# Joining the bf16 products of neighbouring tile pairs in a Strassen-form GEGLU kernel

## Chip, cores, metric

One core of one Trainium2 chip. The metric is the device time of one execution in microseconds (us). Every run quoted here is in the fast state or a single look (state unknown), at a granted clock of 0.999 or 1.0. The **span** of a trace, from its first to its last instruction, is 1.7 to 2.1 us shorter than the time of the same execution in nearly every run.

## The reference, cut

```python
# x 1 x 2048 x 1024, w_gate and w_up 1024 x 3584, w_down 3584 x 1024, all bf16
def reference(x, w_gate, w_up, w_down):
    return (_gelu(x @ w_gate) * (x @ w_up)) @ w_down
```

## The kernel before

The tokens are done in two halves of 1024. A half has a *pair stage* (gate and up products, gelu, multiply) and a *down stage* (times `w_down`). Both replace eight block products by seven, M1 to M7, in the manner of Strassen (Winograd's form). In the pair stage M1 and M2 take bf16 operands as they are; the other five take sums of blocks, kept as 32-bit floats (float32r, printed as f32). Each product is done twice, j = 0 for gate and j = 1 for up, with 4 matmuls of 128x512 each time. One pass handles a *pair* of tiles of the inner dimension; the first half has 12 pairs (numbers 2 to 13), the second 14 (0 to 13).

The kernel uses eight banks of PSUM, the memory that PE writes its products to, in pairs:

```python
PB, VB, QB, RB = (0, 1), (2, 3), (4, 5), (6, 7)

# pair_quads, the seven products; cut: the definitions of mm, prep, add_m5
for j in range(2):                                             # M1, bf16
    mm(PB[j], j, block(key, j, 0, 0), b11, True)
    act(nc.scalar.copy(out=banks[QB[j]][:], in_=banks[PB[j]][:]))
for j in range(2):                                             # M5, f32
    mm(VB[j], j, s(j, "s1"), tsum["t1"], True)
    m5[j] = m_pool.tile([P, TB], F32, name=f"m5_{j}")
    act(nc.scalar.copy(out=m5[j][:], in_=banks[VB[j]][:]))
    prep(j, "s1")            # POOL: the same sum for the next pair
done("m5")                   # hook: other work is issued here
for j in range(2):                                             # M6, f32
    mm(QB[j], j, s(j, "s2"), tsum["t2"], False)
    act(nc.scalar.copy(out=banks[RB[j]][:], in_=banks[QB[j]][:]))
    add_m5(QB[j], QB[j])
    prep(j, "s2")
done("m6")
for j in range(2):                                             # M2, bf16
    mm(PB[j], j, block(key, j, 0, 1), b21, False)
    if j == 0: g[0] = gelu(banks[PB[0]], nxt is None)          # ACT
    else:      mult(hT, g[0], banks[PB[1]], f0, 0)             # DVE
done("m2")
# M7, M3, M4, f32, 8 matmuls each: cut
```

In the first half DVE and the one DMA queue also prepare what later stages read. Four *staging subtractions* a pair, here called A to D, make sums of `w_down` in small buffers and store them to DRAM; two transposed tiles of x a pair go the same way. All these buffers come from one ring of four, handed out in order:

```python
o_pool = ctx.enter_context(tc.tile_pool(name="o", bufs=4))

def stage_step(n):                             # one of A to D
    if k != 1: staged[i].append(o_pool.tile([P, DN], F32R, name="o_sb")[:])
    dve(nc.vector.tensor_tensor(out=t, in0=in0, in1=in1, op=ALU.subtract))
    if k > 0:  sp(nc.sync.dma_start(out=t_dram[:, k - 1, i, :], in_=t.bitcast(F32)))

def stage_x(tb, kd):
    t = o_pool.tile([P, 1, TB], BF16, name="o_sb")
    sp(nc.sync.dma_start_transpose(out=t[:], in_=src))

# where they hang in a pair of the first half
then["m5"] = [lambda q=q: stage_x(*q) for q in xs[:2]]
then["m7"] = [store_x]
then["m3"] = steps[:1] + [lambda i=i: stage_load(i) for i in new]   # A
then["m4"] = steps[1:]                                              # B, C, D
```

(Lines that only choose operands are cut.) B, C and D stand behind M4 of one pair and so run beside the start of the next. Every second pair a new chunk of weights is loaded on the same queue.

## Time and profile before

| quantity | value |
|---|---|
| time, median of the first 3 runs | 543.43 us (543.17 to 544.63) |
| span of the profiled execution | 541.3 us |
| PE / DVE / ACT / POOL busy | 99 / 65 / 48 / 44 % |
| one pair, in both halves | 12.60 us |
| start-up to the first pair | 34.28 us |
| pair stage and down stage, first half | 151.19 and 87.98 us |
| pair stage and down stage, second half | 176.40 and 91.45 us |

The stages are read from the timeline of PE as differences of starts (first pair at 34.28, down stage at 185.47, second half at 273.45, its down stage at 449.85). 99% busy and a chain of PE alone mean that only a shorter stream of matmuls, or a new wait, can move the time.

Two views that the prediction does not show matter later: the staging subtractions (median ns of one is the middle figure of the three), and the DMA queue's issues around pair 9 of the first half, which starts at 122.47 us (start, length, line, what).

```profile
L553 DVE TENSOR_TENSOR o_sb<-wd_sb,o_sb x28: 682/685/1536, 47.9 to 173.9; 128x512 fp32r<-128x512 bf16 x28
```

```profile
113.08 0.33 SPq L555 DMA_DIRECT2D t_dram<-o_sb  x1
113.59 0.38 SPq L161 DMA_DIRECT2D w_mem<-in_w_gate_dram  x1
115.17 6.15 SPq L564 DMA_TRANSPOSE o_sb<-in_x_dram  x2
```

A subtraction takes 0.69 us. Its store goes first, the weights behind it, 8.9 us ahead of pair 9, and the tiles of x behind the weights.

### The profile page before, as it was taken

To read this page: it belongs to the slowest core of one execution; us is meant where nothing else is said; L and a number is where in the kernel's file an instruction comes from. 1 tells how busy PE (TensorE), PEld (TensorE's weight loads), DVE (VectorE), ACT (ScalarE), POOL (GpSimd) and SP (SyncE) were. 2 spreads that over 40 slices of the span, in tenths; PEclk is the share of its full clock that TensorE was granted. 3 is DMA by queue.
4 is the path that set the end of the run, shared out by engine and by line. 5 is a ranking of instruction groups with operands and counts; after the bars stand their busy time and mean duration, and the time that the engine had idled before them with its cause. 6 is when DMAs were issued, how large, how long until landed. Compare 5 with 4: busy or idle time off the path is not lost.

```text
span 541.3 us, 7194 instructions
## 1 busy us (share of the span) xinstructions
PE 534.5 (99%) x2356; PEld 373.1 (69%) x2392; DVE 350.6 (65%) x465; ACT 258.4 (48%) x433; POOL 239.7 (44%) x206
## 2 busy tenths in 40 slices
PE   8999999999999999999999999999999999999997
PEld 4457777776677676767777767777667776866865
DVE  0746666787765999889574444444454469979961
ACT  1435555555555319216455555555555552452270
POOL 0197777888777000000057766677777630000000
PEclk9999999999999999999999999999999999999999
DMA  9956598988836979789952240404040457777946
GB/s 226 306 169 144 183 262 251 173 291 165 278 121 224 347 260 335 217 268 304 311 202 92 64 142 14 156 1 156 0 155 1 157 166 247 249 221 246 289 146 206
DMA packets 85924, 104.80 MB, mean 194 GB/s; under 512 B 18816, under 2 KB 67456, under 8 KB 85888
## 3 DMA queue, kind: packets, MB, share of 16 engines
q1 hardware_dynamic: 84816, 103.83, 62.3%
q10 hardware_dynamic: 1072, 0.52, 0.4%
q8 instruction: 19, 0.31, 0.2%
q14 instruction: 17, 0.14, 0.1%
HBM read 87.03 MB, written 13.63 MB: 186 GB/s over the span
## 4 chain that ended last, share of the span: by engine, by line
PE 97%; DMA 1%; SPq 1%; issue 0%; ACT 0%; ACTq 0%
PE bank L379 60%; PE bank L615 32%; PE bank L245 4%; DMA xT<-in_x_dram 1%; DMA w_mem<-in_w_gate_dram 1%; SPq L172 0%; ACT o_sb L663 0%; SPq L161 0%; ACTq L663 0%
## 5 line engine op out<-in xcount | busy, mean ns | idle before, releaser
L379 PE MATMUL bank<-t_mem,s_mem 128*128 128x512 f32 x1016 | 249.2, 399 | 0.0
L379 PEld LDWEIGHTS bank<-t_mem,s_mem 128*128 128x128 f32 x1016 | 190.9, 188 | 44.1
L353 POOL TENSOR_TENSOR s_mem<-w_mem 128x512 fp32r<-128x512 bf16 x100 | 117.1, 1191 | 197.2 <-DMA w_mem<-in_w_up_dram 105.0
L615 PE MATMUL bank<-t_mem,s_mem 128*128 128x512 f32 x560 | 130.2, 392 | 0.0
L402 DVE TENSOR_TENSOR bank<-bank,m 128x512 f32<-128x512 f32 x104 | 72.1, 698 | 82.8 <-ACT bank L422 74.5
L615 PEld LDWEIGHTS bank<-t_mem,s_mem 128*128 128x128 f32 x560 | 105.1, 188 | 22.9 <-issue 0.2
L269 DVE TENSOR_TENSOR hT<-w_mem,bank 128x512 bf16<-128x512 f32 x104 | 71.3, 687 | 59.1 <-ACT w_mem L264 24.2
L264 ACT ACTIVATE w_mem<-bank 128x512 f32<-128x512 f32 x104 | 61.7, 596 | 80.1 <-DVE bank L402 48.0
L379 PE MATMUL bank<-xT,w_mem 128*128 128x512 bf16 x391 | 97.5, 380 | 1.3
L379 PEld LDWEIGHTS <-w_mem 128*128 128x128 bf16 x416 | 36.6, 98 | 50.4 <-issue 13.3
L528 DVE TENSOR_TENSOR t_mem<-w_mem 128x1024 fp32r<-128x1024 bf16 x56 | 65.6, 1217 | 0.0
L353 POOL TENSOR_TENSOR s_mem<-w_mem,s_mem 128x512 fp32r<-128x512 bf16 x50 | 63.5, 1294 | 0.0
L353 POOL TENSOR_TENSOR s_mem<-s_mem,w_mem 128x512 fp32r<-128x512 f32 x50 | 60.7, 1232 | 0.0
L366 ACT CAST s_mem<-w_mem 128x512 fp32r<-128x512 bf16 x52 | 32.0, 616 | 32.4 <-PE bank L379 28.4
L590 DVE TENSOR_TENSOR s_mem<-hT 128x512 fp32r<-128x512 bf16 x56 | 40.5, 755 | 10.5 <-PE bank L615 7.0
L615 PEld LDWEIGHTS <-hT 128*128 128x128 bf16 x224 | 21.3, 98 | 26.6 <-issue 1.8
L417 ACT COPY m<-bank 128x512 f32<-128x512 f32 x52 | 30.6, 589 | 17.1 <-PE bank L379 17.0
L422 ACT COPY bank<-bank 128x512 f32<-128x512 f32 x52 | 29.6, 570 | 17.0 <-PE bank L379 17.0
L413 ACT COPY bank<-bank 128x512 f32<-128x512 f32 x52 | 29.6, 570 | 13.2 <-PE bank L379 13.2
L663 ACT CAST o_sb<-bank 128x512 bf16<-128x512 f32 x28 | 15.4, 585 | 39.6 <-PE bank L615 39.6
L245 PE MATMUL bank<-xT,w_mem 128*128 128x512 bf16 x125 | 28.0, 379 | 0.8 <-DMA xT<-in_x_dram 0.5
L525 ACT CAST t_mem<-w_mem 128x1024 fp32r<-128x1024 bf16 x28 | 26.9, 1047 | 0.0
(39 smaller groups left out, 230.7 us busy)
## 6 DMA issues: line engine op xcount, KB each, us to landing
t_mem<-t_dram SPq DMA_DIRECT2D x56, 512.0 KB, 5.1
w_mem<-in_w_gate_dram SPq DMA_DIRECT2D x11, 1024.0 KB, 6.4
w_mem<-in_w_up_dram SPq DMA_DIRECT2D x11, 1024.0 KB, 8.6
wd_sb<-in_w_down_dram SPq DMA_DIRECT2D x28, 256.0 KB, 3.9
t_dram<-o_sb SPq DMA_DIRECT2D x28, 256.0 KB, 2.8
wd_sb<-in_w_down_dram SPq DMA_DIRECT2D x12, 512.0 KB, 8.7
w_mem<-in_w_down_dram SPq DMA_DIRECT2D x10, 512.0 KB, 6.6
w_mem<-in_w_down_dram SPq DMA_DIRECT2D x4, 1024.0 KB, 6.7
```

The costliest lines, as they stand in the source:

```text
L245: nc.tensor.matmul(ps[:], lhsT=w_sb[:, kd, fi * P : (fi + 1) * P], rhs=xT[:, kd, tb * TB : (tb + 1) * TB], start=(kd == 0), stop=(kd == KD ...
L264: act(nc.scalar.activation(out=g_sb, in_=ps[:], func=ACT.Gelu_apprx_tanh))
L269: nc.vector.tensor_tensor(out=hT[:, fc, tb * TB : (tb + 1) * TB], in0=g_sb, in1=ps[:], op=ALU.mult,)
L353: pool(nc.gpsimd.tensor_tensor(out=t, in0=in0, in1=in1, op=op))
L366: act(nc.scalar.copy(out=t, in_=a(1, 1)))
L379: nc.tensor.matmul(banks[bank][:], lhsT=lhs[:, c, :], rhs=rhs[:, c, :], start=start and c == 0, stop=c == KH - 1, skip_group_check=True,)
L402: nc.vector.tensor_tensor(out=banks[dst][:], in0=banks[src][:], in1=m5[j][:], op=ALU.add)
L413: act(nc.scalar.copy(out=banks[QB[j]][:], in_=banks[PB[j]][:]))
L417: act(nc.scalar.copy(out=m5[j][:], in_=banks[VB[j]][:]))
L528: dve(nc.vector.tensor_tensor(out=t, in0=in0, in1=in1, op=ALU.subtract))
L590: dve(nc.vector.tensor_tensor(out=t, in0=in0, in1=in1, op=op))
L615: nc.tensor.matmul(banks[bset[u]][:], lhsT=lhs(i, u), rhs=rhs(i), start=start and i == 0, stop=stop and i == NS - 1, skip_group_check=True,)
```

## The change

Each change from bf16 to f32 matmuls was suspected of costing PE some time. M2 of a pair is now held back and runs right behind M1 of the next, so that there is one bf16 run of 16 and one f32 run of 40 a pair. As M2's bank is then still in use when the next M1 needs one, P and V swap roles from pair to pair, and M6 comes ahead of M5 to give that bank time to be read out. The last pair of a half runs both M2s. Core of the diff:

```diff
+        P_, V_ = (PB, VB) if pair % 2 == 0 else (VB, PB)
+        def m2(): ...                 # as before, with P_
+        def do_m5(j): ...             # as before, with V_
+        def do_m6(j): ...             # as before, without add_m5 and prep
         for j in range(2):
-            mm(PB[j], j, block(key, j, 0, 0), b11, True)
+            mm(P_[j], j, block(key, j, 0, 0), b11, True)
...
+        behind = len(pending) > 0
+        if behind:
+            pending.pop()()                     # M2 of the last pair
+        done("m2 of last")
+        if behind:
+            ...
+            order = (do_m6, 0), (do_m6, 1), (do_m5, 0), (do_m5, 1)
+        else:
+            order = (do_m5, 0), (do_m6, 0), (do_m6, 1), (do_m5, 1)
...
         for j in range(2):
+            add_m5(QB[j], QB[j])
+            prep(j, "s2")
         done("m5")
```

Also: the weight chunk is loaded behind "m2 of last" (its old place held the weights that M2 still reads); the b22 cast is done in four pieces in place of one; in last pairs some DMA loads and one DVE piece are issued at other hooks.

More of the change, by code (lines that the diff above doesn't have):

```diff
@@ L239, in t_sum @@
         else:
-            act(nc.scalar.copy(out=t, in_=b(1, 1)))
+            for c in range(KH):
+                act(nc.scalar.copy(out=t[:, c, :], in_=b(1, 1)[:, c, :]))
     def mm_gu(ps, w_sb, fi, tb, kd):
@@ L368 @@
     S_NAMES = ("s1", "s2", "s3", "s4", "a22")
+    pending = []
     def pair_quads(hT, h, pair, nxt, then):
@@ L410, in pair_quads, with m2 @@
         g = {}
-        for j in range(2):
-            mm(PB[j], j, block(key, j, 0, 0), b11, True)
-            act(nc.scalar.copy(out=banks[QB[j]][:], in_=banks[PB[j]][:]))
+        P_, V_ = (PB, VB) if pair % 2 == 0 else (VB, PB)
+        def m2():
+            for j in range(2):
+                mm(P_[j], j, block(key, j, 0, 1), b21, False)
+                if j == 0:
+                    g[0] = gelu(banks[P_[0]], nxt is None)
+                else:
+                    mult(hT, g[0], banks[P_[1]], f0, 0)
@@ new lines, in do_m5, with do_m6 @@
+        def do_m5(j):
+            mm(V_[j], j, s(j, "s1"), tsum["t1"], True)
+            m5[j] = m_pool.tile([P, TB], F32, name=f"m5_{j}")
+            act(nc.scalar.copy(out=m5[j][:], in_=banks[V_[j]][:]))
+            prep(j, "s1")
+        def do_m6(j):
+            mm(QB[j], j, s(j, "s2"), tsum["t2"], False)
+            act(nc.scalar.copy(out=banks[RB[j]][:], in_=banks[QB[j]][:]))
+        for j in range(2):
+            mm(P_[j], j, block(key, j, 0, 0), b11, True)
+            act(nc.scalar.copy(out=banks[QB[j]][:], in_=banks[P_[j]][:]))
@@ new lines, in pair_quads @@
+        behind = len(pending) > 0
[3 more added lines that the diff above has]
+        if behind:
+            if nxt is None:
+                m2()
+                done("m2")
+            else:
+                pending.append(m2)
+            order = (do_m6, 0), (do_m6, 1), (do_m5, 0), (do_m5, 1)
+        else:
+            pending.append(m2)
+            order = (do_m5, 0), (do_m6, 0), (do_m6, 1), (do_m5, 1)
+        for f, j in order:
+            f(j)
+            if (f, j) == (do_m6, 1):
+                done("m6")
@@ L414, in pair_quads @@
         for j in range(2):
-            mm(VB[j], j, s(j, "s1"), tsum["t1"], True)
-            m5[j] = m_pool.tile([P, TB], F32, name=f"m5_{j}")
-            act(nc.scalar.copy(out=m5[j][:], in_=banks[VB[j]][:]))
-            prep(j, "s1")
+            add_m5(QB[j], QB[j])
+            prep(j, "s2")
         done("m5")
         for j in range(2):
-            mm(QB[j], j, s(j, "s2"), tsum["t2"], False)
-            act(nc.scalar.copy(out=banks[RB[j]][:], in_=banks[QB[j]][:]))
-            add_m5(QB[j], QB[j])
@@ L424, in pair_quads @@
-            prep(j, "s2")
-        done("m6")
-        for j in range(2):
-            mm(PB[j], j, block(key, j, 0, 1), b21, False)
-            if j == 0:
-                g[0] = gelu(banks[PB[0]], nxt is None)
-            else:
-                mult(hT, g[0], banks[PB[1]], f0, 0)
-        done("m2")
-        for j in range(2):
             mm(RB[j], j, s(j, "s3"), tsum["t3"], False)
-            add_m5(VB[j], RB[j])
+            add_m5(V_[j], RB[j])
             prep(j, "s3")
             if j == 0:
-                g[1] = gelu(banks[VB[0]], nxt is None)
+                g[1] = gelu(banks[V_[0]], nxt is None)
@@ L439, in pair_quads @@
             else:
-                mult(hT, g[1], banks[VB[1]], f0 + 1, 1)
+                mult(hT, g[1], banks[V_[1]], f0 + 1, 1)
         done("m7")
@@ L782, with load_chunk @@
         for pair in range(first_pair, NPAIR):
+            then = {}
             if pair % PPG == 0 and (pair // PPG + 1) * PPG < NPAIR:
                 key = (h, pair // PPG + 1)
-                if key not in chunks:
+                def load_chunk(key=key):
                     new_chunk(key)
@@ L788 @@
                         load_w(key, j, 0, KD)
-            then = {}
+                if key not in chunks:
+                    then["m2 of last"] = [load_chunk]
             if h == 0:
@@ L800 @@
             if pair == NPAIR - 2:
-                load_wd_rows(0, 4)
-                load_wd_rows(4, 8)
+                then["m2 of last"] = [
+                    lambda: load_wd_rows(0, 4),
+                    lambda: load_wd_rows(4, 8),
+                ]
             if 6 < pair < 11:
@@ L809 @@
             if pair == NPAIR - 1:
-                load_b22(4, 10)
-                load_b22(10, NS)
                 then |= {
+                    "m2 of last": [
+                        lambda: load_b22(4, 10),
+                        lambda: load_b22(10, NS),
+                    ],
                     "m5": [lambda: s_down(hT, 0, "s1", 0, 4)],
-                    "m6": [lambda: s_down(hT, 0, "s1", 4, 8)],
+                    "m6": [
+                        lambda: s_down(hT, 0, "s1", 4, 8),
+                        lambda: t_down(0, "t1", 4, 6),
+                    ],
                     "m2": [
@@ L824 @@
                         lambda: t_down(0, "t2", 0, NT2),
-                        lambda: t_down(0, "t1", 4, 8),
+                        lambda: t_down(0, "t1", 6, 8),
                         lambda: s_down(hT, 0, "s1", 8, NS),
```

## The prediction

> **What bounds the kernel now.** I read the page's busy line first, then the chain that ended last, then the waits, then the timeline of TensorE (PE) in one pair of f tiles.
>
> ```profile
> PE 534.5 (99%) x2356; PEld 373.1 (69%) x2392; DVE 350.6 (65%) x465; ACT 258.4 (48%) x433; POOL 239.7 (44%) x206
> PE 97%; DMA 1%; SPq 1%; issue 0%; ACT 0%; ACTq 0%
> PE bank L379 60%; PE bank L615 32%; PE bank L245 4%; DMA xT<-in_x_dram 1%; DMA w_mem<-in_w_gate_dram 1%; SPq L172 0%; ACT o_sb L663 0%; SPq L161 0%; ACTq L663 0%
> ```
>
> PE is busy 99% of the span and is 97% of the chain; the pair stage (L379), which the change touches, is 60%. In the view of waits PE appears twice only, with 0.8 and 0.5 us, both before the first pair. So there is no wait in the pair stage to remove. What can be gained lies inside "busy". The timeline of PE over one pair, and over the start of the stage after it (start, length, then the group):
>
> ```profile
> 122.47 1.90 PE L379 MATMUL bank<-xT,w_mem 128*128 128x512 bf16 x7
> 124.02 4.00 PE L379 MATMUL bank<-t_mem,s_mem 128*128 128x512 f32 x16
> 127.87 1.90 PE L379 MATMUL bank<-xT,w_mem 128*128 128x512 bf16 x8
> 129.42 5.82 PE L379 MATMUL bank<-t_mem,s_mem 128*128 128x512 f32 x24
> 135.07 1.25 PE L379 MATMUL bank<-xT,w_mem 128*128 128x512 bf16 x4
> ...
> 185.47 6.22 PE L615 MATMUL bank<-w_mem,hT 128*128 128x512 bf16 x27
> 191.34 19.44 PE L615 MATMUL bank<-t_mem,s_mem 128*128 128x512 f32 x84
> 210.62 1.69 PE L615 MATMUL bank<-wd_sb,hT 128*128 128x512 bf16 x6
> ```
>
> I use differences of starts, as lengths overlap in a pipeline. (Some records are missing: a bf16 run of x7 has 8 in the code, x27 has 28.) A pair is M1 (8 bf16 matmuls), M5 and M6 (16 f32), M2 (8 bf16), M7, M3, M4 (24 f32), and lasts 135.07 - 122.47 = 12.60 us. Every pair of the trace has this length within 0.01.
>
> The marginal cost of one matmul comes from a long run less a short one. bf16: (191.34 - 185.47) - (124.02 - 122.47) = 5.87 - 1.55 = 4.32 for 20 more, 0.216 each. f32: (210.62 - 191.34) - (127.87 - 124.02) = 19.28 - 3.85 = 15.43 for 68 more, 0.227 each. At these rates a pair is 16 x 0.216 + 40 x 0.227 = 3.45 + 9.08 = 12.53. So 0.07 us of the 12.60 is lost at the borders between types, of which a pair has two bf16-to-f32 and two back: **some 0.036 us for each bf16 run that stands among f32 ones**. Looking at single starts, it is not a gap: the first six or seven f32 matmuls after a bf16 run stand 0.229 to 0.236 apart.
>
> **What the Trainium skill says.** "TensorE: Matmul & The Clock Gate", section "Wait — 56ns, not 53.3ns?", gives 215.7 ns start to start for warm 512-column matmuls; the bf16 rate here, 0.216 us, agrees, so these are at their floor. The same page, "Weight-path perf modes", says that the fast weight load is on for 128 weights of a type other than FP32. The trace agrees in kind: the page's groups have weight loads of 98 ns for bf16 and 188 ns for f32. That fits a border cost: PE passes from cheap loads to loads nearly as long as a matmul[...]. "Perfetto Trace Analysis", section "Identifying the Most-Contended Engine", warns that matmul busy time does not tell the distance to the limit; here 99% busy indeed hides those 0.07 us a pair. "SBUF — State Buffer", section "Who interferes with whom", says that a VectorE instruction with two SBUF inputs contends with a GpSimd instruction that reads SBUF, one blocking the other for the whole instruction. The trace agrees, and this is my main worry:
>
> ```profile
> 123.52 1.41 DVE L553 TENSOR_TENSOR o_sb<-wd_sb,o_sb 128x512 fp32r<-128x512 bf16 x2
> 126.55 1.67 DVE L553 TENSOR_TENSOR o_sb<-wd_sb 128x512 fp32r<-128x512 bf16 x1 [1.62 <-DMA x_dram<-o_sb]
> 125.38 2.29 POOL L353 TENSOR_TENSOR s_mem<-w_mem 128x512 fp32r<-128x512 bf16 x2 [2.13 <-PE bank L379]
> 127.63 3.18 POOL L353 TENSOR_TENSOR s_mem<-s_mem,w_mem 128x512 fp32r<-128x512 f32 x2
> ```
>
> A staging subtraction (L553) takes 0.7 us while POOL is idle and 1.67 where POOL works; a POOL addition then goes from 1.15 to about 1.6.
>
> **The change, part by part.** *Removed:* no instruction of PE. M2 runs directly behind the next pair's M1, one run of 16 bf16 instead of two of 8. There are 12 pairs in the first half of the tokens and 14 in the second, so 26 x 2 = 52 bf16 runs become 26 (a first pair keeps M1 alone; a last pair has M1 and both M2). 26 x 0.036 = 0.94 us, all of it on the path, as PE is the path.
>
> *New waits of PE in an ordinary pair.* Times from the pair's start, with 0.27 from the nominal end of a product's half to the start of its reader (before, M5's first half ends 2.64 in, POOL starts at 125.38 - 122.47 = 2.91). M1 to 1.73, M2 to 3.46, M6 to 5.30, M5 to 7.11, M7 to 8.92, M3 to 10.74, M4 to 12.56. M6 reads the copies of M1: ACT's second ends at 2.57, M6's second half starts at 4.37: free. M5 writes the bank where M2 lay: its gelu (0.60) ends at 3.47, its multiply (0.69) at 4.42, needed at 5.30 and 6.20: free by 1.8. M3 needs the m5 additions, at 7.8 and 8.7, needed at 8.92 and 9.83: free by 1.1. M4 needs the V addition read out, 9.4, needed at 10.74: free. POOL starts behind M5's first half, at 6.46 instead of 2.91, and with 8 x 1.13 ends 3 us into the next pair; its first result is wanted there at 3.46 and was made second to fourth in that row: free. So with no other work on DVE, no wait comes back, and the second half (14 pairs) should give its 0.5 us in full.
>
> *Added:* the b22 cast in four pieces, some 0.2 us more of ACT (an estimate: four casts of 0.616, overlapping by 0.1, against 1.91 in one). ACT is 48% busy, and early pieces can start before the last region comes free: no cost, perhaps needed so that the first pair of half two, whose M6 is now earlier, doesn't wait. In a last pair M6's DVE work (two of 0.69, one of 1.22 from 6.4 on) comes before the m5 additions: they end near 10.4, the V addition behind two more at 12.2, and M4 needs it at 12.46. Free, by 0.2 to 0.3 only.
>
> Sum without waits: 543.43 - 0.94 = 542.5.
>
> **The rivals.** *A: a wait in the first half, from the shared port.* There DVE does four staging subtractions a pair, three of them around 1.0 to 3.1 into the pair, where POOL now still works: three alternate with POOL's last three, and end near 4.9 instead of 3.1. M2's multiply stands behind them on DVE: 4.9 to 5.6, wanted at 6.2, so still free by 0.6. But these steps also wait for staging buffers: in three pairs (one above, with the 1.62 wait) the last step was held by a store and ended 5.7 to 6.2 into the pair even before. If the delayed steps delay the queue's weight loads and stores by 1 to 1.8 us, the step ends near 6.5 to 7, the multiply near 7.3, and M5's second half stands for 0.3 to 1.2 us, in two pairs, perhaps three; a subtraction with hT behind the m5 additions in four of the pairs could add 0.2 each. This would make it 543.0 to 545. Against it: much of the delay may be taken up by a queue that is backlogged anyway, and the multiply has 1.8 us of room in other pairs.
>
> *B: the border costs nothing that joining saves*, if the slow f32 matmuls come from M5's operands or banks and not from the border: 543.4. Against it: the down stage's long runs are at the marginal rates.
>
> *C: a bf16 run of 16 lets more weight loads go ahead and the f32 start improves further*: 542.2. Nothing in the trace speaks for it, as runs of 8 and 28 show the same start.
>
> *D: weight chunks, now loaded behind M2, come late.* They are asked for some 9 us later in half two, but they land in 6.4 to 8.6 us and are first read more than 20 us later. No effect.
>
> **The number.** 542.5 if nothing waits, which I give 60%; 543 to 545, mean near 543.6, under A with 30%; B and C share the rest. The median lies near 542.7. The three runs before spread from 543.17 to 544.63, which adds a few tenths. Range 542.1 to 544.0. A change of 2% would be 10.9 us; neither the 0.94 nor the largest wait that I can add up comes near it, so within 2% has 0.98, and 0.01 stands on each side.
>
> **What would show it.** Right: pairs of 12.56 us in both halves, a bf16 run of 16 and an f32 run of 40 in each, PE's view of waits still without the pair stage; L553 groups mostly over 1.2 us. A shows as PE waiting for DVE's hT multiply in the first half only, most likely in the pairs after a weight load. B shows as pairs of 12.60 with only one border. The prediction is wrong if the pairs of the second half are not shorter, or if waits of several us come in the last pairs or at the start of the second half.

## The result

Six runs of each kernel on one chip: **543.36 us after (542.38 to 544.53), 543.65 before (543.17 to 544.63)**. Ratio 0.9994, 95% interval 0.9977 to 1.0011: within 2%, and not told apart from no change. A ratio is the mean time of one kernel's fast runs over that of the other's of the same rounds, so it is not quite the ratio of the medians quoted.

The profiled execution is one of the slower ones: 543.97 us, span 542.2. Its busy times and its chain:

```profile
PE 536.0 (99%) x2392; PEld 374.8 (69%) x2392; DVE 360.1 (66%) x465; ACT 258.3 (48%) x439; POOL 245.8 (45%) x206
PE 91%; DMA 5%; DVE 2%; SPq 1%; issue 0%; ACT 0%; DVEq 0%; ACTq 0%
```

Before, PE was 97% of the chain. Now 6 points of it have gone to other engines. Busy time says nothing: 99% both times. The timeline of PE, three pairs of the second half, and pair 9 of the first half:

```profile
310.31 3.63 PE L382 MATMUL bank<-xT,w_mem 128*128 128x512 bf16 x16
313.59 9.44 PE L382 MATMUL bank<-t_mem,s_mem 128*128 128x512 f32 x40
322.87 2.33 PE L382 MATMUL bank<-xT,w_mem 128*128 128x512 bf16 x10
```

```profile
120.51 3.63 PE L382 MATMUL bank<-xT,w_mem 128*128 128x512 bf16 x16
123.79 3.10 PE L382 MATMUL bank<-t_mem,s_mem 128*128 128x512 f32 x12
127.72 6.89 PE L382 MATMUL bank<-t_mem,s_mem 128*128 128x512 f32 x28 [0.83 <-DVE hT L270]
134.45 1.90 PE L382 MATMUL bank<-xT,w_mem 128*128 128x512 bf16 x8
```

A pair without a wait lasts 322.87 - 310.31 = **12.56 us, 0.04 less than before**. So does each pair of the second half between its first and its last, and each of the first half but one. In pair 9 the f32 part stops after 12 matmuls and takes 134.45 - 123.79 = 10.66 in place of 9.28, **1.38 us more**, waiting for a multiply into hT, M2's. (The 0.83 in brackets is the idle time by modelled ends; the difference of runs is what the wait cost.) The view of waits names both that and a second place, in a down stage:

```profile
PE bank L382 <- DVE hT L270: 0.8, 1, 0.8
PE bank L642 <- DMA t_mem<-t_dram: 0.2, 1, 0.2
```

By stages, from starts as before (the last column is the span):

| execution | start-up | pairs 1 | down 1 | pairs 2 | down 2 | span |
|---|---|---|---|---|---|---|
| before | 34.28 | 151.19 | 87.98 | 176.40 | 91.45 | 541.3 |
| after | 34.33 | 152.09 | 87.94 | 175.84 | 92.00 | 542.2 |
| difference | +0.05 | +0.90 | -0.04 | -0.56 | +0.55 | +0.9 |

The first half gains 0.48 and loses 1.38; the second gains 0.56. The +0.55 is in a stage whose order the change doesn't touch. The gain of the borders is 1.04 in all, and two waits eat it in this execution.

**Where the wait in pair 9 comes from.** DVE and POOL around the start of pair 9 (120.51 us), then pieces of the chain that leads to the wait, in order of time ("..." marks pieces left out):

```profile
121.61 2.61 DVE L580 TENSOR_TENSOR o_sb<-wd_sb,o_sb 128x512 fp32r<-128x512 bf16 x2
126.37 0.69 DVE L580 TENSOR_TENSOR o_sb<-wd_sb 128x512 fp32r<-128x512 bf16 x1 [2.16 <-DMA x_dram<-o_sb]
126.98 0.68 DVE L270 TENSOR_TENSOR hT<-w_mem,bank 128x512 bf16<-128x512 f32 x1
```

```profile
122.06 3.18 POOL L354 TENSOR_TENSOR s_mem<-w_mem,s_mem 128x512 fp32r<-128x512 bf16 x2
```

```profile
111.69 1.55 DVE o_sb L580
...
113.26 0.33 SPq L582
...
113.77 0.38 SPq L161
...
114.95 9.58 DMA o_sb<-in_x_dram
...
124.60 1.75 DMA x_dram<-o_sb
...
126.37 0.04 DVE o_sb L580
...
126.98 0.69 DVE hT L270
...
127.72 0.50 PE bank L382
```

Read it from the top. In pair 8, D (1.55 us, beside POOL) ends; its store is issued, then the weights, then a transposed tile of x, which lands at 124.53 and is stored; that store lands at 126.35 and frees a ring buffer; D of pair 9 takes it; M2's multiply stands behind D on DVE; PE waits for that multiply to free a bank. The subtractions are slow because POOL's additions now start behind M5 late in the pair and reach into the next:

```profile
L580 DVE TENSOR_TENSOR o_sb<-wd_sb,o_sb x28: 683/1182/1545, 46.2 to 173.2; 128x512 fp32r<-128x512 bf16 x28
```

The median went from 685 to 1182 ns. In pair 8, D ends 5.3 us after the pair's start; before it was 3.2 (113.08 less 109.87, where pair 8 began). So the weights go out 6.74 us ahead of pair 9 in place of 8.88, and the x store lands 5.84 us into the pair in place of 4.05. In absolute time that queue stands where it stood (weights at 113.77 against 113.59). What moved is the pair: it starts 1.95 us earlier, 1.73 of it because M2 of the last pair now lies behind that start. The subtractions hang on the pair's start and would have come earlier too; the collisions took just that away. And M2's multiply, which had until the next pair's M1, now has until M5's second half, 6.2 us into the pair.

### The profile page after: what moved, and what is told of

It reads as the page before. It is cut to its first block, busy times and chain, and to the rows that moved or that the text cites. A ratio compares the mean times of both kernels' runs of the same rounds, so it can differ in the third digit from the quotient of the medians.

```text
span 542.2 us, 7130 instructions
## 1 busy us (share of the span) xinstructions
PE 536.0 (99%) x2392; PEld 374.8 (69%) x2392; DVE 360.1 (66%) x465; ACT 258.3 (48%) x439; POOL 245.8 (45%) x206
## 4 chain that ended last, share of the span: by engine, by line
PE 91%; DMA 5%; DVE 2%; SPq 1%; issue 0%; ACT 0%; DVEq 0%; ACTq 0%
PE bank L382 56%; PE bank L642 31%; PE bank L246 4%; DMA o_sb<-in_x_dram 2%; DMA t_mem<-t_dram 1%; DVE o_sb L580 1%; DMA xT<-in_x_dram 1%; DMA w_mem<-in_w_gate_dram 1%; SPq L172 0%; DVE bank L405 0%; DVE hT L270 0%; DMA x_dram<-o_sb 0%; SPq L161 0%; DVE s_mem L617 0%; ACT m L427 0%
## 5 line engine op out<-in xcount | busy, mean ns | idle before, releaser
L382 PE MATMUL bank<-t_mem,s_mem 128*128 128x512 f32 x1016 | 240.4, 394 | 0.8 <-DVE hT L270 0.8
L354 POOL TENSOR_TENSOR s_mem<-w_mem 128x512 fp32r<-128x512 bf16 x100 | 119.0, 1208 | 192.5 <-DMA w_mem<-in_w_up_dram 103.7
L642 PE MATMUL bank<-t_mem,s_mem 128*128 128x512 f32 x560 | 130.4, 393 | 0.2 <-DMA t_mem<-t_dram 0.2
L405 DVE TENSOR_TENSOR bank<-bank,m 128x512 f32<-128x512 f32 x104 | 68.2, 694 | 56.5 <-ACT m L427 52.0
L382 PE MATMUL bank<-xT,w_mem 128*128 128x512 bf16 x416 | 94.3, 380 | 0.0
L382 PEld LDWEIGHTS <-w_mem 128*128 128x128 bf16 x416 | 38.7, 98 | 49.7 <-issue 6.5
L354 POOL TENSOR_TENSOR s_mem<-w_mem,s_mem 128x512 fp32r<-128x512 bf16 x50 | 65.9, 1337 | 0.0
L354 POOL TENSOR_TENSOR s_mem<-s_mem,w_mem 128x512 fp32r<-128x512 f32 x50 | 63.1, 1280 | 0.0
L617 DVE TENSOR_TENSOR s_mem<-hT 128x512 fp32r<-128x512 bf16 x56 | 38.0, 712 | 8.5 <-PE bank L642 7.6
L690 ACT CAST o_sb<-bank 128x512 bf16<-128x512 f32 x28 | 15.4, 585 | 39.6 <-PE bank L642 39.6
L580 DVE TENSOR_TENSOR o_sb<-wd_sb,o_sb 128x512 fp32r<-128x512 bf16 x28 | 32.9, 1175 | 1.1 <-DMA x_dram<-o_sb 0.7
L246 PE MATMUL bank<-xT,w_mem 128*128 128x512 bf16 x128 | 28.1, 379 | 0.9 <-DMA xT<-in_x_dram 0.6
```

Source lines behind the costliest of these rows:

```text
L246: nc.tensor.matmul(ps[:], lhsT=w_sb[:, kd, fi * P : (fi + 1) * P], rhs=xT[:, kd, tb * TB : (tb + 1) * TB], start=(kd == 0), stop=(kd == KD ...
L354: pool(nc.gpsimd.tensor_tensor(out=t, in0=in0, in1=in1, op=op))
L382: nc.tensor.matmul(banks[bank][:], lhsT=lhs[:, c, :], rhs=rhs[:, c, :], start=start and c == 0, stop=c == KH - 1, skip_group_check=True,)
L405: nc.vector.tensor_tensor(out=banks[dst][:], in0=banks[src][:], in1=m5[j][:], op=ALU.add)
L617: dve(nc.vector.tensor_tensor(out=t, in0=in0, in1=in1, op=op))
L642: nc.tensor.matmul(banks[bset[u]][:], lhsT=lhs(i, u), rhs=rhs(i), start=start and i == 0, stop=stop and i == NS - 1, skip_group_check=True,)
```

## The experiments

Kernels sent together shared one chip and 11 runs of the kernel before on it. "Wait in pair 9" is the length of its f32 run less 9.28 us.

### 1. The changed kernel again, twice

Edit: none (5 rounds for a_again, one look for a_third).

> The changed kernel once more, unchanged, for a second trace and more times. Theory (border saving of 0.037 us a pair, 0.96 us in all, taken back by one wait in pair 9 of the first half, 1.38 us in the trace at hand, and by late landings of t_mem rows in the down stage, 0.5 us there): pairs of 12.56 us again, a wait before M5's second half in pair 9 of between 0 and 1.5 us, times in two groups some 1.5 us apart, mean ratio to before 0.998 to 1.0005. Rival (the wait in pair 9 was an accident of one profiled execution): no wait in pair 9, and a ratio of 0.998 throughout.

> A third look at the changed kernel, as its wait in pair 9 was 1.38 us in one trace and 0.10 in the other. Theory: the wait follows the landing of the x stores; in pair 9 M5's second half starts about 1.3 us after the landing of the store that D needs, wherever that lies beyond 4.9 us. Rival: wait and landing have nothing to do with each other.

Measured: 543.17 us (542.34 to 545.06, 6 runs) against 543.64; ratio 0.9992 (0.9974 to 1.0009). The second look took 542.65. In the three traces of the same program the wait in pair 9 was **1.38, 0.10 and 0**. a_again's profiled execution was nevertheless the slowest of all, 545.06, span 543.2, by other places:

```profile
PE bank L642 <- DMA t_mem<-t_dram: 1.0, 1, 1.0
PE bank L296 <- DMA w_mem<-in_x_dram: 0.5, 1, 0.5
```

Its start-up took 35.94 us, 1.6 more than in the other two, and a down stage lost 1.31 to a load of the sums that M4 reads from DRAM. Both are outside what the change touches. All 13 executions of the changed kernel fall into two heaps: seven from 542.34 to 542.75 and six from 543.65 to 545.06. Only two of the upper heap have a trace, and they lost their time at different places, so what makes the heaps stays open. In all three traces the gate weights are asked for 6.7 us ahead of pair 9; only the landings differ: they take 7.5, 6.3 and 5.6 us from issue to landing, the first x tile behind them 9.6, 8.6 and 7.9. The x store lands 5.84, 4.81 and 4.17 us into the pair, in the order of the waits. The trace of experiment 7, which leaves these pairs as they are, gives a fourth point: 5.32, and a wait of 0.86. Where the landing is late, M5's second half starts 1.37 us behind it both times (127.72 - 126.35, and 128.18 - 126.81), as the theory for a_third had it. In all four D starts within 0.03 us of the landing. Why equal loads differ so from execution to execution stays open.

### 2. Subtractions moved out of POOL's way (x_defer)

```diff
                 then["m3"] = steps[:1] + [lambda i=i: stage_load(i) for i in new]
-                then["m4"] = steps[1:]
...
+            then["m2 of last"] = then.get("m2 of last", []) + held
+            held = steps[1:] if h == 0 else []
```

B, C and D now run behind M2's multiply in the next pair, where POOL has stopped.

> The changed kernel with the last three staging subtractions of a pair (B, C, D) moved behind the multiply of M2 in the next pair; the weight load is then also ahead of their stores in the queue. Theory: M2's multiply ends near 4.4 us into the pair in all pairs, no PE wait in pair 9 or anywhere in the pair stage, every pair 12.56; the subtractions then run while POOL is idle and mostly take 0.7 us instead of 1.2 on average; time 0.96 us (0.2%) below before, some 542.6, ratio 0.998. Rival (the wait comes from the DMA queue as such, and something else will wait in its place): a PE wait of about 1 us remains in the first half, on another DVE instruction, ratio near 1.000.

Measured: **542.62 us (542.29 to 543.87, 6 runs) against 543.64, ratio 0.9981 (0.9968 to 0.9993)**. PE and DVE at the start of pair 9, 120.57 us:

```profile
124.31 0.69 DVE L270 TENSOR_TENSOR hT<-w_mem,bank 128x512 bf16<-128x512 f32 x1 [1.44 <-PE bank L382]
124.91 1.41 DVE L580 TENSOR_TENSOR o_sb<-wd_sb,o_sb 128x512 fp32r<-128x512 bf16 x2
```

The multiply starts as soon as PE has the product, 3.7 us into the pair; behind it two subtractions take 1.41 us, 0.7 each. Their median over the stage is 692 ns. Every pair lasts 12.56 and there is no wait in the pair stage. That agrees with the theory, but two things changed at once, the collision and the order on DVE. In this order the multiply stands ahead of B, C and D, so it cannot wait for their buffers. The next run keeps the order.

### 3. Collision kept, buffer freed (x_sep)

```diff
+    xo_pool = ctx.enter_context(tc.tile_pool(name="xo", bufs=1))
...
-        t = o_pool.tile([P, 1, TB], BF16, name="o_sb")
+        if kd % 2:
+            t = xo_pool.tile([P, 1, TB], BF16, name="xo_sb")
+        else:
+            t = o_pool.tile([P, 1, TB], BF16, name="o_sb")
```

Every second tile of x has a buffer of its own, so that D no longer takes the buffer of the late store. (A larger ring for all would have been a plainer test; none was run.)

> The changed kernel with every second transposed x tile in a buffer of its own, so that the last subtraction D of a pair no longer needs the buffer of an x tile whose store lands late. The order of all engines is as in the changed kernel. Theory (the wait in pair 9 is D held by the store of x): the subtractions still collide with POOL (mean near 1.2 us), but D of pair 9 ends near 5 us into the pair instead of 6.5, and PE does not wait: time as in the deferred version within 0.3 us. Rival (the collision with POOL alone is enough to make PE wait): PE still waits in pair 9, 0.5 us or more.

Measured: **542.58 us (542.10 to 543.22, 5 runs) against 543.64, ratio 0.9982 (0.9968 to 0.9996)**. DVE in pair 9, which starts at 120.56:

```profile
124.19 1.65 DVE L581 TENSOR_TENSOR o_sb<-wd_sb 128x512 fp32r<-128x512 bf16 x1
125.77 0.68 DVE L271 TENSOR_TENSOR hT<-w_mem,bank 128x512 bf16<-128x512 f32 x1
```

D still collides, 1.65 us, but starts at 124.19, ahead of the landing of the x store at 124.66, and no subtraction of this trace waits for a buffer. The multiply ends 5.9 us into the pair and M5's second half comes at 6.2: no wait. So a collision on DVE alone costs PE nothing here. What this trace does not show is that the buffer of its own removed a wait: its x store landed early, 4.10 us into the pair, and in a_third, with the old ring, a landing at 4.17 let the multiply end at 5.9 too. That **the ring buffer held by a late store makes the wait** rests on the four traces of experiment 1: one order of work, and a wait that follows the landing. The intervals of x_defer and x_sep overlap with that of the changed kernel (0.9974 to 1.0009), so their times alone don't tell them from it.

### 4. The link through the queue (x_storelate, x_storelate2)

```diff
-            sp(nc.sync.dma_start(out=t_dram[:, k - 1, i, :], in_=t.bitcast(F32)))
+            store = lambda: sp(nc.sync.dma_start(out=dst, in_=t.bitcast(F32)))
+            if later is None: store()
+            else:             later.append(store)     # issued at "m2 of last"
```

The subtractions keep their place; only the stores of B to D are issued behind the next load of weights, which then needn't wait for them.

> The changed kernel with DVE's order untouched; only the stores of the results of B, C and D are issued later, behind the weight load of the next pair. It tests the middle link of the chain: that the subtractions, late through POOL, hold back the weight load in the queue, this the transposed x tiles behind it, and these the buffer that D of pair 9 needs. Theory: the weight load of pair 8 is issued near 3 to 4 us into the pair instead of 5.8, the x stores land some 2 us earlier, D of pair 9 starts near 4 to 4.5 instead of 5.86, M2's multiply ends by 6.0, and PE's wait in pair 9 is 0 to 0.2 us; ratio to before near 0.998. Rival (lateness of the multiply comes from the collision itself, whatever the queue does): PE waits in pair 9 as in the changed kernel.

> A second look at the version with only the stores late, as its times spread from 542.0 to 545.2. Theory: PE waits in the pair stage 0 to 0.3 us in all, and what more the execution takes over 540.3 us of span lies in the down stage. Rival: a wait of over 0.5 us stands in the pair stage again.

Measured: 542.93 us (542.01 to 545.20, 6 runs) against 543.63, ratio 0.9992 (0.9976 to 1.0007), unclear. In the first trace the gate weights go out 9.61 us ahead of pair 9, the x store lands 3.49 us into it and the wait is 0.03: as the chain has it. In the second (542.78) they go out 9.61 us ahead again, but take 8.1 us; the x store lands at 4.85 and the wait is 0.55, over the 0 to 0.3 that was expected. This wait is another one. DVE in pair 9, which starts at 120.72:

```profile
122.62 0.91 DVE L580 TENSOR_TENSOR o_sb<-wd_sb 128x512 fp32r<-128x512 bf16 x1 [2.57 <-DMA t_dram<-o_sb]
```

This is A, held 2.57 us by one of the stores that the edit put behind the weights (issued at 112.41, landed at 122.60); D does not wait here. In the first trace A stood for 1.25 us in the same way. So the early stores did hold the weights back, 9.61 against 6.74 us; that earlier weights make the x store land earlier was seen in one trace of two; and the edit brought a wait of its own.

### 5. The cost of a border, measured by itself (b_border)

The kernel *before*, with M2's two halves parted, one ahead of M7 and one behind it: one more border each way in every pair, and no other change of work.

```diff
+        mm(PB[0], 0, block(key, 0, 0, 1), b21, False)
+        g[0] = gelu(banks[PB[0]], nxt is None)
         for j in range(2):                              # M7
...
+        mm(PB[1], 1, block(key, 1, 0, 1), b21, False)
+        mult(hT, g[0], banks[PB[1]], f0, 0)
```

> The kernel before with M2's two halves taken apart: the first between M6 and M7, the second between M7 and M3, so that a pair has three bf16 runs (8, 4 and 4) instead of two, and nothing else. Theory (each bf16 run among f32 ones costs 0.036 us): pairs of 12.637 us instead of 12.600, 26 x 0.037 = 0.96 us more in all, no PE wait. Rival (the slow f32 matmuls belong to M5's and M7's operands or banks, not to the border): pairs stay at 12.600.

Measured: 545.61 us (545.39 to 545.77, 4 runs) against 543.64, ratio 1.0032 (1.0019 to 1.0046). One pair in the timeline of PE:

```profile
99.73 4.00 PE L379 MATMUL bank<-t_mem,s_mem 128*128 128x512 f32 x16
103.58 1.04 PE L379 MATMUL bank<-xT,w_mem 128*128 128x512 bf16 x4
104.26 2.21 PE L379 MATMUL bank<-t_mem,s_mem 128*128 128x512 f32 x8
106.31 1.04 PE L379 MATMUL bank<-xT,w_mem 128*128 128x512 bf16 x4
```

The pair lasts 12.68, which is 0.08 more, twice what was expected; 26 x 0.08 = 2.1, and the medians differ by 1.97. The f32 run of 8 takes 106.31 - 104.26 = 2.05 us: at the 0.227 of a long run it would take 1.82. The sign and the kind are as the theory has them, and the rival that a border costs nothing falls. The size misses: the cost of a border is no constant. Above the 12.53 that the prediction's rates give, a pair with one, two and three bf16 runs takes 0.03, 0.07 and 0.15. In single starts the f32 matmuls of the run of 8 stand 0.224 to 0.239 apart to its end, and the run behind it has nine slow ones (up to 0.236), where a run behind 8 bf16 has six. Why is not settled.

### 6. Is M6 ahead of M5 needed? (x_m5first)

```diff
-            order = (do_m6, 0), (do_m6, 1), (do_m5, 0), (do_m5, 1)
+            order = (do_m5, 0), (do_m5, 1), (do_m6, 0), (do_m6, 1)
```

> The changed kernel with M5 in front of M6 again, M2 moved as in the change: M5's second half then wants the bank of M2's multiply 4.4 us into the pair instead of 6.2. Theory: in the second half of the tokens the multiply ends at 4.4 and the wait is 0 to 0.1 us a pair; in the first half POOL starts 1.8 us earlier and the collisions end earlier, but D held by the x store in pairs 7 and 9 leaves waits of about 1 us each, so 1.5 to 4 us more than the deferred version, 544 to 546.5 in all. Rival (the order of M5 and M6 does not matter): as the changed kernel, 543.2 within 0.5.

Measured: **558.38 us (557.16 to 559.71, 4 runs) against 543.63, ratio 1.0278 (1.0263 to 1.0293)**. Both theories missed, by far. One ordinary pair of the second half, which starts at 330.72:

```profile
334.26 9.63 PE L382 MATMUL bank<-t_mem,s_mem 128*128 128x512 f32 x40
343.74 0.61 PE L382 MATMUL bank<-xT,w_mem 128*128 128x512 bf16 x2
```

The pair lasts 13.02 us, 0.46 more, in both halves. The first f32 matmul starts 3.54 into the pair in place of 3.28: the gelu that frees its bank ends at 3.40. Later M7 starts at 7.45, behind M6's copy (ended 7.30). Each link is two or three tenths, but it returns in every pair, and there is always a next one. The last pairs lose 1.67 each. In the second half 12 x 0.46 + 1.67 = 7.2, and its pair stage is 7.15 longer than after. In the first half pair 3 waits for M2's multiply besides and lasts 13.94. The expectation had counted only such waits. How the 0.46 divides among the links was not settled.

### 7. The b22 cast in one piece (x_b22one)

```diff
-            for c in range(KH):
-                act(nc.scalar.copy(out=t[:, c, :], in_=b(1, 1)[:, c, :]))
+            act(nc.scalar.copy(out=t, in_=b(1, 1)))
```

> The changed kernel with the b22 cast in one piece again. Theory: the cast ends some 1.2 us into the first pair of the second half, the two output casts and the copies of M1 follow on ACT, and M6's first half, now at 2.66 us, waits 0.05 to 0.3 us for its copy; no other pair changes. Rival: no wait, the split is without use for time.

Measured, one look: 544.37 us. ACT around the start of the second half, at 274.77 here:

```profile
274.06 1.91 ACT L240 CAST t_mem<-xT 128x2048 fp32r<-128x2048 bf16 x1 [2.10 <-DMA w_mem<-in_w_gate_dram]
276.81 1.08 ACT L435 COPY bank<-bank 128x512 f32<-128x512 f32 x2
```

The one cast starts when the last region is free and holds up the copies of M1 that M6 reads. The first f32 runs of that half take 9.47 us together against 9.28 with four pieces: 0.19 lost, inside the 0.05 to 0.3 expected. The same trace has waits in pair 5 (0.58) and pair 9 (0.86), with the x store of pair 9 landing at 5.32. The total of one look says nothing on 0.19 us.

### 8. An attempt to beat both (x_best)

x_defer and x_sep together, and in the down stage the loads of `b21` held until PE has done all of M6, to clear the queue for the sums that M6 waits for:

```diff
-            if i == 4:
+            if i == 12:
                 for q in range(4):
-                    load_b21(n, q)
+                    load_b21(n, q, last_on["pe"] if q == 0 else None)
```

> The changed kernel with the subtractions deferred behind M2's multiply, every second x tile in its own buffer, and in the down stage the b21 weights held until M6 is nearly done, so that the four t2 transfers, whose last rows M6 needs some 17.2 us into a down group and which landed there between 16.0 and 18.3, have the DMA engines for themselves. Theory (what spread is left comes from those landings): the last t2 transfer lands near 14 to 15.5 us into the group, no PE wait in the down stage, a time of 542.2 to 542.5 with a narrow spread, ratio 0.997 to 0.998. Rival (the landings depend on the transfers in front of them, not on b21 behind): landings as before, 542.6 with the same spread.

Measured: 544.15 us (543.45 to 545.14, 6 runs) against 543.39, ratio 1.0015 (1.0002 to 1.0027): 0.15% slower, within 2%. There is no wait in the pair stage, but the down stage has a new one:

```profile
PE bank L650 <- DMA t_mem<-t_dram: 0.2, 1, 0.2
```

The sums for M6 landed hardly earlier (15.4 to 16.3 us into a group; the 18.3 of the expectation stands in none of the traces kept, whose latest is 17.5). The later sums for M4, behind the held loads, slipped in the first half to 34.35 and 31.2 us, from 29.5 and 27.1 in x_sep. Two waits of 0.47 and 0.25 us appear there in the first half, and 0.7 fell in the start-up. The wait only changed places. **x_defer and x_sep, one alone, remain the best that was run**, 0.2% under the kernel before, with intervals that leave out 1.

## Why the prediction was right or wrong

**Right: the class, the bound and the gain of the borders.** Within 2%, as it had to be. The time of 543.36 lies in the range, 0.66 over the median forecast and 0.86 over the sum of 542.5. The range (542.1 to 544.0) also holds the 543.65 of before, so the hit is in part luck: neither it nor the ratio tells a gain from none. The pairs do. The border step (0.036 us, 26 runs, 0.94) measured 0.04 a pair and 1.04 in sum, the pairs 12.56 to the hundredth; that a constant cost was good enough here is luck too, as b_border shows (0.08 for one more run). The second half shows 175.84 us in all of the executions of the changed kernel and of x_defer and x_sep that were profiled. Where no wait comes the whole gain is there: x_sep's span is 540.3, 1.0 under the 541.3 of before, and the ratios of x_defer and x_sep, 0.19% and 0.18% of 543.6, are 1.0 us each.

**Right: rival A's mechanism.** It said that subtractions would collide with POOL, delay the queue, and bring the step to 6.5 to 7 and the multiply to 7.3 us. Measured in pair 9: D ends at 6.55, the multiply at 7.15, in the first half only, and in a pair after a weight load. The weights went out 2.14 us later against the pair, over the "1 to 1.8", the x store landed 1.79 later, and the wait came to 0 to 1.38, around the "0.3 to 1.2". Where nothing holds D, the multiply ended at 5.9 and not at 5.6, so the room was 0.3 and not 0.6. It hit one pair in the changed kernel's own traces, not two or three. The prediction read three pairs in which a buffer had held the last step to 5.7 or later before; the trace has two, 7 and 9, and in pair 7 it was the step before the last that waited. The added 0.2 from subtractions with hT was not seen.

**Wrong: A as one of two cases.** The step "542.5 if nothing waits, which I give 60%; 543 to 545 under A with 30%" treats the wait as a property of the kernel, there or not. The three traces of one program gave 1.38, 0.10 and 0: each execution draws anew. With the wait averaging some 0.5 in them (an estimate from three), about half the gain was given back; the ratios of the two sets of six, 0.06% and 0.08%, are gains of 0.3 and 0.4 us, which agrees in size, though neither interval leaves out 1. A mean, not a choice of branch, was what had to be predicted.

**Missed: the edges outside the change.** The prediction put the spread of the times before down as "a few tenths". It is start-up (34.3 to 35.9 us) and the down stages, where the last of four loads of sums lands 15.4 to 17.5 us into a group in the traces kept, and M6 reads it at some 17.2. In the trace of before they landed at 15.7 to 16.6, so the chain had no DMA wait to show, though the slack was 0.6. In the changed kernel's traces these edges cost up to 2.9 us (a_again, 1.6 and 1.31), enough to hide an effect of 1 us. The kernel before has a single trace, without them; its times spread as widely (542.96 to 545.03), for a cause not shown.

**The other rivals.** B (the border costs nothing) fell by b_border and by the pairs of 12.56. C (more gain with runs of 16) fell too: 12.56 is what the sum gave. D (late weights) had no effect by itself; the weights matter only as what stands ahead of the x tiles. The last pairs, "free, by 0.2 to 0.3 only", were free. The four pieces of the b22 cast were needed, for 0.19. Why a border costs PE time (the prediction tied it to the weight loads, 98 against 188 ns) no run tests.

**What the skill gave.** "SBUF — State Buffer", section "Who interferes with whom", states the lock between a VectorE instruction with two SBUF inputs and GpSimd's reads; the trace after agrees (685 to 1182 ns in the median). It foretold the collision rightly; x_sep shows that the collision alone makes PE wait for nothing, with 0.3 us to spare.

## What to carry to other kernels

Where matmuls of two types alternate, each border can cost some hundredths of a microsecond that the profile books as busy: compare long and short runs, and group by type. Before moving a product to another place, follow what hangs on it: here the helper engine's row moved into another engine's row, and through a store, an in-order queue and a ring of four buffers this reached the matmuls again. When the last link is a DMA landing, take several traces of the same program before naming a cost, and look for the buffer that was held.

## What the Trainium skill lacked or had wrong

- "TensorE: Matmul & The Clock Gate" has no float32r rate and no cost for passing from bf16 to float32r matmuls. Here 128x512 float32r matmuls took 0.227 us with weight loads of 188 ns, and a bf16 run among them cost 0.04 us a pair; parting it in two of 4 cost 0.08 more.
- The same page, section "Back-to-back issue gap", gives about 131 ns as the sustained spacing at N=512. No run here shows it: bf16 stood at 0.216 us in runs of up to 28, as the page's other figure, 215.7 ns, has it.
- "SBUF — State Buffer", section "Who interferes with whom": the lock is as stated, with alternating turns (0.69 us to as much as 1.67). The page does not say that the larger effect can be on a DMA queue behind it: weights issued 2.14 us later against the pair, a wait of up to 1.38.
- No page that was read says how much equal loads, issued at the same point, vary between executions of one program: the gate weights, 1 MB asked for at the same point, took 5.6, 6.3 and 7.5 us, and PE waited 0, 0.10 and 1.38.
